# Fused attention and gated layers on one core: filler matmuls get steps and PSUM banks of their own

## Chip, cores, metric

One core of a Trainium2 chip. The metric is the device time of one execution in microseconds (us); three timed executions of the kernel before gave 471.35 us (median), 470.24 and 474.1 us.

## What is computed

The reference, cut to what matters (batch 8, 8 heads, 576 rows, head width 64, 32 packed rows, float32):

```python
def sm_attn(qq, kk, vv):
    s = scale * np.matmul(qq, kk.transpose(0, 1, 3, 2))
    s = s - np.max(s, axis=-1, keepdims=True)
    a = np.exp(s)
    a = a / (np.sum(a, axis=-1, keepdims=True) + 1e-09)
    return np.matmul(a, vv)
p_packed = sm_attn(p, k, v)
out = sm_attn(q, p_packed, p_packed)
...
x = np.ascontiguousarray(attn_out.transpose(0, 2, 1, 3)).reshape(B * S, H * D)
h = np.maximum(np.maximum(x @ w1, x @ w2), x @ w3)
return (h @ w_out).astype(np.float32)
```

## The kernel before

The work goes batch by batch (`b` 0 to 7). For a batch, `scores` multiplies the packed queries with the keys (line 255, `s<-kt`), `weigh` takes the maximum on VectorE (line 268) and the exponential on ScalarE (line 273), `turn` transposes the result on TensorE (lines 298 and 299, `tp`), `values` multiplies by the values (line 346), `packed` transposes the 32 packed rows (line 361), `queries` multiplies them with the queries (line 375, `s<-q`), `attend` does the second softmax, its scores being transposed out of PSUM by VectorE (line 398, `e<-s`). `project` multiplies the packed rows with the three first-layer weights of one block of 128 hidden columns (line 448, `pw`), split into a high part by ScalarE (line 459, `ph`) and a low part by VectorE (line 461, `pl`). `layer_in` applies that to the second softmax (line 484, `mi`: the bulk of the time), `maximum` combines the three sums, and `layer_out` does the output layer (line 553, `mo`).

`convert` unpacks the first-layer weights, which arrive as 64-bit words, in four steps: two on ScalarE (lines 190 and 195), one on VectorE (line 204), one on GpSimd (line 208).

The order of all work is written out by hand. Two strings are read word by word, START (batches 0 and 1 and the beginning of 2: the ramp) and LOOP (each further batch); nothing else orders the program. A word is one step of a stage. The first letter names the stage: `S` scores, `A` weigh and turn, `V` values, `K` packed, `Q` queries, `B` attend, `P` project, `N` layer_in, `E` maximum, `C` convert; digits are the batch and its part. Small letters issue loads on SyncE's queue (`k10` the keys of batch 1, first half; `w02` weights of block 0, part 2; `v`, `q` likewise). Each engine runs its own instructions in that order, so an instruction that waits holds up all behind it on its engine.

PSUM is given out from two pools: `ps_big` with two slots of two banks (scores, query scores, most projections) and `ps_moe` with four slots of one bank, tag `moe` (the layers' sums `mi` and `mo`, and, for batch 0, `tp`, `pa` and the first projection). A slot is given to a new tile when the last step that used the old tile stands earlier in the order; the first matmul of the new tile then waits for that step's instruction.

TensorE also does idle products, matmuls of the identity with itself that nobody reads. In the kernel before, a word `I10` only notes a number; the next stage that calls `rouse` issues that many products of 128 columns (at most four to a matmul) into the tile it is about to fill itself:

```python
if kind == "I":
    idle[0] = int(name[1:])
    continue
```

So the idle products wait for whatever that tile waits for, and stand between the wait and the stage's own matmuls. START has eight such words: I10 before `S0`, I10 and I1 before the two transposes of batch 0, I9 before `V00`, I2 before `Q0`, I5 before `S1` (the scores of batch 1), I3 before `S2`, I1 before `V101`.

Of the kernel before, what the change touches and what calls it, by code (L numbers as in the profile page):

```python
# [10 lines left out]
F32 = mybir.dt.float32  # L11
# [11 lines left out]
P = 128  # L23
# [22 lines left out]


START = """
k00 k01 I10 S0 A01 A01 I10 A01 A00 A00 v01 w00 C00 q010 v00 q000 A01 I1 A00 A00v C00 C00 I9 V00 Z00 q001 V00
V01 Z01 V01 K0 w01 K0v C01 I2 Q0 B010 B010 q011 Q0 C01 k11 k10 C01 B001 B001 B000 B011 B000 B011 w02 B000v  # L50
B011v C00 k21 B010 C01 B010 B010 B000 B000 B000v I5 S1 B011 k20 w12 C02 C02 I3 S2 B001 A10 B001 C02 C02 P00
B010v A11 A10 A11 B011 B010 B011 C12 B000 P00 B010g Z10 C12 B011 B010 w11 B010v B000g B000 v10 B001 A21 B001v
P00 P00 A11 Z11 B001 A20 B001g B011g B000v w10 v11 B000v A21 A10 B001 q10 C12 B001v A20 C10 N00 w21 B011 B010v
A10 A11 I1 V101 C10 B011 P00 N00 V101 C11 C11 B001v C11 C12 E000 q11 N00 C21 K1 C21 w20 N00 C10 K1v Q1 E000
E000 C20 C20 C21 w22 Z20 B011 N00 w30 B10 C22 C11 C10 P01 P01 N00 E001 w31 B11 B11 C21 C20 C20 C22 C22 C22 w50
C30 P01 w32 B10 C31 C30 P10 w41 X2 B10v N01 E010 C30 N01 C31 P02 P02 C31 w40 C32 N01 E001 E010 E001 C30 N01
N01 E011 C32 B11 C31 P02 C32 C32 E010 N02 v21 E011 N02 v20 N02 N02 w42 w52 B10 X2 H00 E020 E020 E020 B11 B11
B11v C40 C40 C40 C40 C41 C41 P03 N02 C41 P03 E021v P03 N01 N02 E021 w51 C42 C42 N03 N03 B10 X2 C41 B11 C52 B10
P10 w64 E011 C50 N03 C42 C42 E030v P10 H00 B10 Z21 N03 C52 P04 B11g P11 P04 E031 E021 E030 P04 N03 B10g w62
C52 N03 E030 N04 N04 E031 B11 C51 C51 B10 E040 E031 C52 E040 w65 H00 C50 B11 B11v P11 C51 N04 N04 B10 B10v N04  # L60
N04 E041 C64 C64 E041 E041 E040 C51 N10 C62 H02v E100 N10 N10 C50 C50 V201 q20 P11 P05 H03v w63 H02 C65 C65
C65 N11 E110 C64 C64 H03v C65 N11 N10 E100 V201 K2 E110 P05 C62 W2 N10 P05 E100 E101v C62 w60 H02v C63 N11
E110 H03v K2 q21 Q2 B21 N05 N05 C63 C63 B20 H01 E050 C63 N10 B20 B20 C60 P13 E050 W2 E101 C60 E101 P12 P13 W2
N05 H04v N05 P13 E050 C62 N11 E111 C60 N11 E111 B20 N11 W1v H03v P12 W1 P12 N13 E111 E051 N05 E051 H04 N05 N12
E051 C60 E130 N13 W1 N13 N12 W2 W2v P15 w61 C61 C61 C61 E120v E120 E130 P14 W1 W1v N13 C61 W0v W0v N12 E120
N12 W2 N13 H05g N12 W2 W2 P15 E130 H03 N12 E131 P15 B21 E121 E121 E131 P14 P14 N15 N15 N15 W0 N13 E150 E150
N14 N14 W2 N14 N14 N15 N15 E121 H03v H05 W2 W0 W0v E131 N14 W1 E150 E140 E140 E140 W0 W0 W0 H13 H04v H05 B20
E151v B20 O0 N14 E141v E141 E151 W1v N15 H01v E141 W0 k30 O0 F0 H10 O0 F0 O0 O0 O0 E151 H05v H10 W1 k31 P20
B20 H01 F0 H01v F0 W0v H10v P21 H05 B21v F0 H01 H05v P22 H01v F0 H12 H11 H14v O0 W1g H11v O0 H11v P21 B21 F0
O0 O0 H13 P20 P20 P20 H11v F0 H12 H12v B20 O0 F0 F0 F0 F0 H13 W1v P20 O0 B20 O0 O0 H14 F0 H14v F0 F0 B21 O1 F0  # L70
H15 H15v H15 O1 H11 B21 H13v F1 F1 H15v H15 H13v P22 O1 F1 H11v O1 H13v H15v O1 B20 F1 O1 O1 B20 O1 F1 B21
B21g P21 O1 O1 F1 F1 F1 F1 F1 F1 F1 P22 B21 O1 F1 O1 O1 F1 B21 B21 F1 O1 F1
"""


# [13 lines left out]
def fused_kernel(ctx: ExitStack, tc: tile.TileContext, kp, qt, va, vb, wi, wo, out):  # L89
# [19 lines left out]
    ps_moe = ctx.enter_context(tc.tile_pool(name="ps_moe", bufs=4, space=PSUM))  # L109
# [3 lines left out]
    ident = const.tile([P, P], F32, name="ident")  # L113
# [21 lines left out]
    def split_lo(lo, src, hi, default="g"):  # L135
        on(default).tensor_tensor(out=lo, in0=src, in1=hi.bitcast(F32), op=ALU.subtract)  # L136

    idle = [0]

    def rouse(ps):  # L140

        k = ps.shape[-1] // P
        for i in range(0, idle[0], k):
            n = min(idle[0] - i, k)
            nc.tensor.matmul(  # L145
                out=ps[:, 0:n * P], lhsT=ident, rhs=ident.unsqueeze(1).to_broadcast([P, n, P]),
                start=True, stop=True,
            )
        idle[0] = 0


    staged, loaded = {}, {}
    def load_w(j, c):
# [89 lines left out]
    s1, a1, z1, a1t, av, pp, s2, a2 = {}, {}, {}, {}, {}, {}, {}, {}  # L243

    def scores(b):

        kt = [loaded.pop(("k", b, g)) for g in range(G)]
        s1[b] = [ps_big.tile([P, 2, 512], F32, name=f"s1_{b}_{r}", tag="big") for r in range(R)]
        rouse(s1[b][0][:, 0])
        for hf in range(2):  # L250
            for n, (g, pr) in enumerate(QUADS):
                for r in range(R):
                    o = slice(64 * r, 64 * r + 64)
                    w = 2 * S + 64 * pr + 32 * r
                    nc.tensor.matmul(  # L255
                        out=s1[b][r][32 * n:32 * n + 32, hf, 0:HS],
                        lhsT=kt[g][o, w:w + NP],
                        rhs=kt[g][o, pr * S + hf * HS:pr * S + (hf + 1) * HS],
                        start=True, stop=True,
                    )  # L260
        yield 0
# [26 lines left out]
    def turn(b, r):  # L288
        if b == 0:
            tp = ps_moe.tile([P, 512], F32, name=f"tp{b}_{r}", tag="moe")  # L290
            pa = ps_moe.tile([P, 512], F32, name=f"pa{b}_{r}", tag="moe")
        else:
            x = ps_big.tile([P, 2, 512], F32, name=f"tp{b}_{r}", tag="big")
            tp, pa = x[:, 0], x[:, 1]
        a = a1[b, r][0]
        rouse(tp)
        for t in range(SF):
            nc.tensor.transpose(out=tp[:, t * P:(t + 1) * P], in_=a[:, t * P:(t + 1) * P], identity=ident)  # L298
        nc.tensor.transpose(out=pa[0:SR, 0:P], in_=a[:, SF * P:S], identity=ident)
        yield 2  # L300
        at = pool.tile([P, SF + 1, P], F32, name=f"a1t{b}_{r}", tag="b", bufs=NB)
        copy(at[:, 0:SF, :], tp.rearrange("p (t x) -> p t x", x=P))
        copy(at[0:SR, SF, :], pa[0:SR, 0:P])
        a1t[b, r] = at.rearrange("p t (i y) -> p t i y", y=NP)
        av[b, r] = pa
# [27 lines left out]
    def values(b, rs):  # L333

        at = {r: a1t.pop((b, r)) for r in rs}
        if (b, 0) not in av:
            x = ps_big.tile([P, 2, 512], F32, name=f"av{b}", tag="big")
            for r in range(R):
                av[b, r] = x[:, r]
        ps = {r: av[b, r][:, P:P + D] for r in rs}  # L340
        rouse(av[b, rs[0]][:, P:4 * P])
        for t, r in [(t, r) for ts in (range(SF), (SF,)) for r in rs for t in ts]:
            n = P if t < SF else SR
            for i, (g, pr) in enumerate(QUADS):
                h = 2 * pr + r
                nc.tensor.matmul(  # L346
                    out=ps[r][NP * i:NP * i + NP, :],
                    lhsT=at[r][0:n, t, i],
                    rhs=loaded["v", b, g][0:n, t, h * D:(h + 1) * D],
                    start=(t == 0), stop=(t == SF),  # L350
                )
        yield 1
        if b not in pp:
            pp[b] = pool.tile([P, R, D], F32, name=f"pp{b}", tag="pp", bufs=2)
        for r in rs:
            nc.vector.tensor_scalar(out=pp[b][:, r], in0=ps[r], scalar1=z1[b, r], scalar2=None, op0=ALU.mult)
# [8 lines left out]
    def queries(b):  # L365

        q = [loaded["q", b, g] for g in range(G)]
        s2[b] = []
        for hf in range(2):
            s2[b].append(ps_big.tile([P, R, 512], F32, name=f"s2_{b}_{hf}", tag="big"))  # L370
            rouse(s2[b][hf][:, 0])
            for n, (g, pr) in enumerate(QUADS):
                for r in range(R):
                    o = slice(64 * r, 64 * r + 64)
                    nc.tensor.matmul(  # L375
                        out=s2[b][hf][32 * n:32 * n + 32, r, 0:HS],
                        lhsT=pt_sb[b % 2][o, NP * n:NP * n + NP], rhs=q[g][o, pr, hf * HS:(hf + 1) * HS],
                        start=True, stop=True,
                    )
            if b == 0 or hf == 1:  # L380
                yield 0
# [51 lines left out]
    def project(b, j):  # L433
# [7 lines left out]
        else:  # L441
            x = ps_big.tile([P, R, 512], F32, name=f"pw{b}_{j}", tag="big")
            ps, src = [x[:, r] for r in range(R)], [x[:, :, 0:NW * P]]
        rouse(ps[0])
        for n in range(4):
            for r in range(R):
                o = slice(64 * r, 64 * r + 64)
# [20 lines left out]
    def layer_in(b, j):  # L468
# [3 lines left out]
        for hf in range(2):  # L472
            c = slice(hf * HS, (hf + 1) * HS)
            for i in range(NW):
                new = (range(NW) if i == 0 else ()) if first else (i,)
                for x in new:
                    sums[b, j, hf, x] = ps_moe.tile([P, 512], F32, name=f"mi{b}_{j}_{hf}_{x}", tag="moe")
                rouse(sums[b, j, hf, i])

                steps = [((2 * i + x) % 3, (2 * i + x) // 3) for x in range(2)] if first else [(i, 0), (i, 1)]  # L480
                for x, r in steps:
# [146 lines left out]
    def run(words, base):  # L628

        for word in words.split():  # L630
            name = word.rstrip("vga")
            chosen[0] = word[len(name):] or None
            kind, x = name[0], [int(i) for i in name[1:]]
            if kind == "I":
                idle[0] = int(name[1:])
                continue
            if kind not in "wCW":
                x[0] += base
# [58 lines left out]
```

## Time and profile before

| | us |
|---|---|
| median of 3 timed executions | 471.35 |
| lowest, highest of them | 470.24, 474.1 |
| the profiled execution, its own time | 474.43 |
| the span of the profiled execution | 472.7 |
| TensorE busy in that span | 457.1 |

The span runs from the first instruction to the last; 1.73 us of the profiled execution's time lie outside it. The profile says for each engine how long it was busy and what ended each of its idle times. The granted clock is TensorE's, as a share of 2.4 GHz: 1.00 is that level, 0.50 is 1.2 GHz.

### The profile page before, as it was taken

The numbers are of one execution on the slowest core, as the hardware profiler recorded it, in microseconds if no ns is written. First come the engines' busy times: TensorE is split into PE (matmuls) and PEld (weight loads), VectorE is DVE, ScalarE is ACT, GpSimd is POOL, SyncE is SP. The second block draws the span as 40 slices with busy tenths as digits, with TensorE's granted clock in tenths as the row PEclk, the third lists the DMA queues.
The fourth block names the chain that finished last, engine by engine and source line by source line (L and its number), as shares of the span: only waits on it lengthen the run. The fifth ranks groups of instructions, "written<-read, shape, count | busy, mean of one in ns | idle before, by whom it ended". The sixth has DMA issues, their size and how long they took to land.

```text
span 472.7 us, 11472 instructions
## 1 busy us (share of the span) xinstructions
PE 457.1 (97%) x4714; PEld 405.6 (86%) x4714; DVE 350.5 (74%) x763; ACT 171.8 (36%) x333; POOL 207.0 (44%) x180
## 2 busy tenths in 40 slices
PE   8769999999999999999999999999999999999996
PEld 4337887989899898989989898998989899898996
DVE  1677999999986678786777678786787767875652
ACT  3256876563441226122350224312260223402330
POOL 0335865766244046512564037521556036531642
PEclk9958999999999999999999999999999999999999
DMA  8995968003024730075102741057100910020002
GB/s 298 404 382 184 278 238 323 2 1 112 26 75 146 249 120 3 25 249 184 58 1 82 270 116 49 26 182 249 59 3 25 323 56 3 25 76 1 2 0 101
DMA packets 25540, 59.20 MB, mean 125 GB/s; under 512 B 2448, under 2 KB 15760, under 8 KB 25488
## 3 DMA queue, kind: packets, MB, share of 16 engines
q1 hardware_dynamic: 25488, 58.47, 36.3%
q8 instruction: 37, 0.61, 0.5%
q14 instruction: 15, 0.12, 0.1%
HBM read 45.48 MB, written 12.98 MB: 124 GB/s over the span
## 4 chain that ended last, share of the span: by engine, by line
PE 90%; DVE 4%; DMA 4%; ACT 1%; issue 1%; SPq 0%; DVEq 0%; ACTq 0%
PE mi L484 46%; PE mo L553 28%; PE pw L448 6%; PE s L255 2%; PE av L346 2%; PE s L375 2%; DMA wi<-in_wi 1%; DMA q<-in_qt 1%; DMA kt<-in_kp 1%; PE s L145 1%; DVE w_sb L204 1%; PE tp L145 1%; PE tp L298 1%; DVE e L398 1%; DVE xt L220 0%
## 5 line engine op out<-in xcount | busy, mean ns | idle before, releaser
L484 PE MATMUL mi<-a2h,ph 128*128 128x288 f32 x576 | 174.3, 303 | 0.7 <-ACT r L131 0.5
L484 PE MATMUL mi<-a2h,pl 128*128 128x288 f32 x576 | 170.3, 296 | 0.4 <-DVE pl L461 0.4
L484 PE MATMUL mi<-a2l,ph 128*128 128x288 f32 x576 | 170.2, 295 | 0.0
L484 PEld LDWEIGHTS mi<-a2h,ph 128*128 128x128 f32 x576 | 108.4, 188 | 16.1 <-issue 7.0
L484 PEld LDWEIGHTS mi<-a2h,pl 128*128 128x128 f32 x576 | 108.5, 188 | 0.6 <-DVE pl L461 0.6
L484 PEld LDWEIGHTS mi<-a2l,ph 128*128 128x128 f32 x576 | 108.4, 188 | 0.0
L498 DVE TENSOR_TENSOR r<-mi,r 128x288 f32<-128x288 f32 x192 | 83.3, 449 | 33.3 <-PE mi L484 31.2
L131 ACT COPY r<-mi 128x288 f32<-128x288 f32 x60 | 23.4, 400 | 123.3 <-PE mi L484 123.3
L461 DVE SCALAR_TENSOR_TENSOR pl<-pw,ph 128x768 fp32r<-128x768 f32 (+1 forms) x61 | 46.8, 775 | 3.9 <-ACT ph L459 3.0
L459 ACT ACTIVATE ph<-pw 128x768 fp32r<-128x768 f32 (+1 forms) x61 | 39.9, 675 | 21.8 <-PE pw L448 18.1
L553 PE MATMUL mo<-ych,xl 128*128 128x288 f32 x144 | 42.5, 295 | 0.0
L553 PE MATMUL mo<-ych,xh 128*128 128x288 f32 x144 | 42.4, 295 | 0.0
L553 PE MATMUL mo<-ycl,xh 128*128 128x288 f32 x144 | 42.4, 294 | 0.0
L136 POOL TENSOR_TENSOR yal<-r,yah 128x576 fp32r<-128x576 f32 x13 | 18.6, 1429 | 46.1 <-ACT yah L131 46.1
L448 PE MATMUL pw<-w_sb,pt 64*32 64x384 f32 x768 | 36.5, 495 | 1.0 <-POOL w_sb L208 1.0
L208 POOL TENSOR_TENSOR w_sb<-w_sb,wi 128x512 int32<-128x512 int32 x18 | 24.2, 1349 | 28.0 <-DVE z L284 11.7
L273 ACT ACTIVATE a<-s,nm 128x576 f32<-128x576 f32 x16 | 11.9, 743 | 67.3 <-DVE nm L269 67.1
L522 POOL TENSOR_TENSOR r<-r 128x288 f32<-128x288 f32 (+1 forms) x25 | 27.8, 1127 | 17.5 <-issue 9.0
L133 POOL CAST yah<-r 128x576 fp32r<-128x576 f32 x6 | 4.0, 663 | 57.0 <-DVE r L522 57.0
L553 PE MATMUL mo<-yah,xh 128*128 128x288 f32 x96 | 28.8, 300 | 0.0
L133 DVE COPY r<-mi 128x288 f32<-128x288 f32 x36 | 16.3, 455 | 16.2 <-PE mi L484 16.2
L553 PE MATMUL mo<-yal,xh 128*128 128x288 f32 x96 | 28.3, 295 | 0.0
(121 smaller groups left out, 883.6 us busy)
## 6 DMA issues: line engine op xcount, KB each, us to landing
kt<-in_kp SPq DMA_DIRECT2D x16, 640.0 KB, 4.7
wi<-in_wi SPq DMA_DIRECT2D x18, 512.0 KB, 7.0
v<-in_va SPq DMA_DIRECT2D x16, 512.0 KB, 5.9
q<-in_qt SPq DMA_DIRECT2D x14, 576.0 KB, 6.9
xk<-x SPq DMA_DIRECT2D x6, 576.0 KB, 4.9
wi<-in_wo SPq DMA_DIRECT2D x6, 512.0 KB, 5.7
out_t<-r SPq DMA_DIRECT2D x8, 288.0 KB, 2.2
out_t<-t SPq DMA_DIRECT2D x8, 288.0 KB, 2.3
```

Source lines behind the costliest of these rows:

```text
L131: e.copy(out=out, in_=src)
L133: e.tensor_copy(out=out, in_=src)
L136: on(default).tensor_tensor(out=lo, in0=src, in1=hi.bitcast(F32), op=ALU.subtract)
L208: nc.gpsimd.tensor_tensor(out=dst.bitcast(I32), in0=dst.bitcast(I32), in1=up, op=ALU.add)
L273: nc.scalar.activation(out=a.rearrange("p (a b) -> p a b", a=2), in_=s[:, :, 0:HS], func=AF.Exp, bias=nm, scale=SCALE, accum_out=z,)
L448: nc.tensor.matmul(out=ps[r][NP * n:NP * n + NP, 0:NW * P], lhsT=pt_sb[b % 2][o, NP * n:NP * n + NP], rhs=w_sb[o, j, n * NW * P:(n + 1) * ...
L459: nc.scalar.activation(out=hi[:, r], in_=x, func=AF.Copy, scale=2.0 ** -WS)
L461: nc.vector.scalar_tensor_tensor(out=lo[:, r], in0=x, scalar=2.0 ** -WS, in1=hi[:, r].bitcast(F32), op0=ALU.mult, op1=ALU.subtract,)
L484: nc.tensor.matmul(out=sums[b, j, hf, x][:, 0:HS], lhsT=w[:, r, x * P:(x + 1) * P], rhs=a[:, c], start=(r == 0 and n == 0), stop=(r == R - ...
L498: nc.vector.tensor_tensor(out=h, in0=sums[b, j, hf, i][:, 0:HS], in1=h, op=ALU.max)
L522: less = lambda out, x, y: on("g").tensor_tensor(out=out, in0=x, in1=y, op=ALU.subtract)
L553: nc.tensor.matmul(out=ps[:, 0:HS], lhsT=w[:, x, m * P:(m + 1) * P], rhs=h[:, z], start=(p == 0 and i == 0), stop=(p == NQ - 1 and i == 2),)
```

## The change

`rouse` and its calls go (lines 140 to 149 and the six stages that call it). A word `J<n>` takes their place and is a step of its own: it issues its products at once, each into a new tile of the pool `ps_moe`, 512 columns at most:

```diff
-    idle = [0]
-
-    def rouse(ps):
-        k = ps.shape[-1] // P
-        for i in range(0, idle[0], k):
-            n = min(idle[0] - i, k)
+    def doze(n):
+        for i in range(0, n, 4):
+            k = min(n - i, 4)
+            ps = ps_moe.tile([P, 512], F32, name=f"idle{len(dozes)}", tag="moe")
+            dozes.append(ps)
             nc.tensor.matmul(
-                out=ps[:, 0:n * P], lhsT=ident, rhs=ident.unsqueeze(1).to_broadcast([P, n, P]),
+                out=ps[:, 0:k * P], lhsT=ident, rhs=ident.unsqueeze(1).to_broadcast([P, k, P]),
                 start=True, stop=True,
             )
-        idle[0] = 0
+    dozes = []
...
-            if kind == "I":
-                idle[0] = int(name[1:])
+            if kind == "J":
+                doze(int(name[1:]))
                 continue
```

```diff
-k00 k01 I10 S0 A01 A01 I10 A01 A00 A00 v01 w00 C00 q010 v00 q000 A01 I1 A00 A00v C00 C00 I9 V00 Z00 q001 V00
+k00 k01 J10 S0 A01 A01 J7 A01 A00 A00 v01 w00 C00 q010 v00 q000 A01 A00 A00v C00 C00 J1 V00 Z00 q001 V00 V01 Z01
```

START now has J10 before `S0`, J7 before the first transpose of batch 0, J1 before `V00`, before `K0`, before `Q0` and between the two halves of `Q0`, J11 before `S1`, J12 before `S2`, J8 and J1 before the two transposes of batch 1, J1 before `Q1`, J2 before the projection `P01`, J6 before `N01` (the second layer block of batch 0). Together 62 products of 128 columns where 41 stood. All other words keep their order, on every engine and on the load queue, and LOOP is unchanged.

TensorE's rows before the values of batch 0 (`pa<-v`), with the semaphores that they wait for, before and after:

```order
L299 MATMUL pa_0_147<-ident,a_0_0_127 64x128
L145 MATMUL pa_0_147<-ident 128x384 [waits DVE_49]
L145 MATMUL pa_0_147<-ident 128x384 x2
L346 MATMUL pa_0_147<-v_138,a1t_0_154 32x64 [waits DMAHW6_49]
L346 MATMUL pa_0_147<-v_138,a1t_0_154 32x64
```

```order
L296 MATMUL pa_0_151<-ident,a_0_0_131 64x128 [waits PE_49]
L144 MATMUL idle_162<-ident 128x128 [waits Activation_49]
L342 MATMUL pa_0_151<-v_142,a1t_0_157 32x64 [waits DMAHW6_49,DVE_49]
L342 MATMUL pa_0_151<-v_142,a1t_0_157 32x64
L342 MATMUL pa_0_151<-v_134,a1t_0_157 32x64 [waits DMAHW2_49]
```

Three matmuls, 1152 columns, went; one of 128 columns stands there, and the wait for VectorE's copy (`DVE_49`) moved from the first idle product to the first product of the values.

TensorE's rows from the second half of the query scores of batch 0 (`s<-q`) to the scores of batch 1 (`s<-kt`), before and after:

```order
L375 MATMUL s_0_1_232<-q_136,pt_75 32x288 [waits DMAHW3_49]
L375 MATMUL s_0_1_232<-q_136,pt_75 32x288 x3
L145 MATMUL s_1_0_273<-ident 128x512 [waits DVE_49,PE_49]
L145 MATMUL s_1_0_273<-ident 128x128
L255 MATMUL s_1_0_273<-kt_244 32x288 [waits DMAHW5_49]
L255 MATMUL s_1_1_274<-kt_244 32x288 [waits DVE_49,PE_49]
```

```order
L370 MATMUL s_0_1_239<-q_140,pt_75 32x288 [waits DMAHW3_49]
L370 MATMUL s_0_1_239<-q_140,pt_75 32x288 x3
L144 MATMUL idle_280<-ident 128x512 [waits PE_49]
L144 MATMUL idle_282<-ident 128x512 [waits PE_49]
L144 MATMUL idle_284<-ident 128x384
L253 MATMUL s_1_0_286<-kt_251 32x288 [waits DMAHW5_49,DVE_49,PE_49]
L253 MATMUL s_1_1_287<-kt_251 32x288 [waits DVE_49,PE_49]
```

The idle products (640 columns, now 1408) no longer stand behind the wait for VectorE (its transposes out of the slot that the scores take); they wait only for earlier idle products of TensorE itself, and the scores carry the wait.

TensorE's rows from the projection of batch 1 (`pw_0_616`, then `pw_0_641`) to the block `N01` (`mi_1_0_0`), before and after:

```order
L448 MATMUL pw_0_616<-w_sb,pt_76 32x384 [waits DVE_49,PE_49]
L448 MATMUL pw_0_616<-w_sb,pt_76 32x384 x7
L484 MATMUL mi_1_0_0_633<-a2h_0_400,ph_1_583 128x288 [waits Activation_49]
L484 MATMUL mi_1_0_0_633<-a2h_0_400,pl_1_584 128x288 [waits DVE_49]
L484 MATMUL mi_1_0_0_633<-a2l_0_407,ph_1_583 128x288
```

```order
L442 MATMUL pw_0_641<-w_sb,pt_76 32x384 [waits DVE_49,PE_49]
L442 MATMUL pw_0_641<-w_sb,pt_76 32x384 x7
L144 MATMUL idle_658<-ident 128x512 [waits PE_49]
L144 MATMUL idle_660<-ident 128x256 [waits Activation_49]
L477 MATMUL mi_1_0_0_662<-a2h_0_420,ph_1_608 128x288 [waits PE_49]
L477 MATMUL mi_1_0_0_662<-a2h_0_420,pl_1_609 128x288 [waits DVE_49]
```

Two idle products, 768 columns, stand where none stood; the second waits for the ScalarE copy that frees its bank, for which the block's second sum waited before.

## Rows read from the trace of the kernel before

**Rows 1.** The page: span, TensorE's busy time, its granted clock in 40 slices.
```profile
span 472.7 us, 11472 instructions
...
PE 457.1 (97%) x4714; PEld 405.6 (86%) x4714; DVE 350.5 (74%) x763; ACT 171.8 (36%) x333; POOL 207.0 (44%) x180
...
PEclk9958999999999999999999999999999999999999
```

**Rows 2.** Windows: length, busy us by engine (instructions), granted clock, DMA share, GB/s.
```profile
18.40:22.10 3.70, 1.36 (x14) 0.78 (x20) 3.63 (x11) 0.46 (x2) 2.65 (x3) 1.00 1.03 413
22.10:39.20 17.10, 12.85 (x164) 7.67 (x163) 12.43 (x37) 11.52 (x27) 6.09 (x7) 0.50 0.97 362
...
48.00:60.00 12.00, 12.00 (x113) 10.20 (x105) 11.56 (x28) 9.84 (x18) 9.54 (x9) 1.00 0.92 289
...
100.00:200.00 100.00, 99.78 (x957) 93.19 (x957) 81.44 (x164) 35.29 (x68) 45.43 (x40) 1.00 0.27 89
```

**Rows 3.** Timeline of TensorE in the ramp: start, us, what [idle before <-releaser].
```profile
12.14 2.20 PE L145 MATMUL pa<-ident 128*128 128x384 f32 x6 [0.86 <-DVE a1t L133]
14.27 1.73 PE L346 MATMUL pa<-v,a1t 128*32 128x64 f32 x80
...
17.21 1.21 PE L375 MATMUL s<-q,pt 64*32 64x288 f32 x32
20.75 1.32 PE L145 MATMUL s<-ident 128*128 128x512 f32 x4 [2.34 <-DVE e L398]
22.00 2.10 PE L255 MATMUL s<-kt 64*32 64x288 f32 x32
26.07 1.65 PE L145 MATMUL s<-ident 128*128 128x384 f32 x2 [1.97 <-ACT a L273]
27.64 2.17 PE L255 MATMUL s<-kt 64*32 64x288 f32 x32
29.57 1.53 PE L448 MATMUL pw<-w_sb,pt 64*32 64x384 f32 x16
33.38 1.11 PE L298 MATMUL tp<-ident,a 128*128 128x128 f32 x4 [2.28 <-ACT a L273]
...
37.57 2.22 PE L346 MATMUL tp<-v,a1t 128*32 128x64 f32 x80
...
42.41 1.20 PE L375 MATMUL s<-q,pt 64*32 64x288 f32 x32
...
45.58 0.88 PE L448 MATMUL pw<-w_sb,pt 64*32 64x384 f32 x16 [0.97 <-POOL w_sb L208]
...
47.39 0.88 PE L448 MATMUL pw<-w_sb,pt 64*32 64x384 f32 x16
48.20 0.40 PE L484 MATMUL mi<-a2h,ph 128*128 128x288 f32 x1
```

**Rows 4.** Timeline of SyncE, ScalarE and VectorE in the ramp, same columns.
```profile
9.81 1.13 SPq L161 DMA_DIRECT2D kt<-in_kp  x2
...
12.22 0.33 SPq L155 DMA_DIRECT2D wi<-in_wi  x1
...
22.80 0.66 ACT L190 ACTIVATE wi<-wi 128x512 f32<-128x512 f32 x1
...
25.18 0.74 ACT L273 ACTIVATE a<-s,nm 128x576 f32<-128x576 f32 x1 [0.83 <-DVE nm L269]
...
26.46 0.74 ACT L273 ACTIVATE a<-s,nm 128x576 f32<-128x576 f32 x1 [0.45 <-DVE nm L269]
...
33.47 0.74 ACT L273 ACTIVATE a<-s,nm 128x576 f32<-128x576 f32 x1
...
41.93 0.94 DVE L498 TENSOR_TENSOR r<-mi,r 128x288 f32<-128x288 f32 x2
```

**Rows 5.** DMA issues of 10.2 to 11.5 us, then 12 to 16: KB, us to landing.
```profile
kt<-in_kp SPq DMA_DIRECT2D x1, 640.0 KB, 9.7
...
wi<-in_wi SPq DMA_DIRECT2D x1, 512.0 KB, 9.3
```

More of the change, by code (lines that the diff above doesn't have):

```diff
@@ L48 @@
 START = """
-k00 k01 I10 S0 A01 A01 I10 A01 A00 A00 v01 w00 C00 q010 v00 q000 A01 I1 A00 A00v C00 C00 I9 V00 Z00 q001 V00
[L50 to L72, printed above, removed]
+k00 k01 J10 S0 A01 A01 J7 A01 A00 A00 v01 w00 C00 q010 v00 q000 A01 A00 A00v C00 C00 J1 V00 Z00 q001 V00 V01 Z01
@@ new lines @@
+V01 J1 K0 w01 K0v C01 J1 Q0 B010 B010 q011 J1 Q0 C01 k11 k10 C01 B001 B001 B000 B011 B000 B011 w02 B000v B011v
+C00 k21 B010 C01 B010 B010 B000 B000 B000v J11 S1 B011 k20 w12 C02 C02 J12 S2 B001 A10 B001 C02 C02 P00 B010v
+A11 A10 A11 B011 B010 B011 C12 B000 P00 B010g Z10 C12 B011 B010 w11 B010v B000g B000 v10 B001 A21 B001v P00 P00
+J8 A11 Z11 B001 A20 B001g B011g B000v w10 v11 B000v A21 J1 A10 B001 q10 C12 B001v A20 C10 N00 w21 B011 B010v A10
+A11 V101 C10 B011 P00 N00 V101 C11 C11 B001v C11 C12 E000 q11 N00 C21 K1 C21 w20 N00 C10 K1v J1 Q1 E000 E000 C20
@@ new lines @@
+C20 C21 w22 Z20 B011 N00 w30 B10 C22 C11 C10 J2 P01 P01 N00 E001 w31 B11 B11 C21 C20 C20 C22 C22 C22 w50 C30 P01
+w32 B10 C31 C30 P10 w41 X2 B10v J6 N01 E010 C30 N01 C31 P02 P02 C31 w40 C32 N01 E001 E010 E001 C30 N01 N01 E011
+C32 B11 C31 P02 C32 C32 E010 N02 v21 E011 N02 v20 N02 N02 w42 w52 B10 X2 H00 E020 E020 E020 B11 B11 B11v C40 C40
+C40 C40 C41 C41 P03 N02 C41 P03 E021v P03 N01 N02 E021 w51 C42 C42 N03 N03 B10 X2 C41 B11 C52 B10 P10 w64 E011
+C50 N03 C42 C42 E030v P10 H00 B10 Z21 N03 C52 P04 B11g P11 P04 E031 E021 E030 P04 N03 B10g w62 C52 N03 E030 N04
@@ new lines @@
+N04 E031 B11 C51 C51 B10 E040 E031 C52 E040 w65 H00 C50 B11 B11v P11 C51 N04 N04 B10 B10v N04 N04 E041 C64 C64
+E041 E041 E040 C51 N10 C62 H02v E100 N10 N10 C50 C50 V201 q20 P11 P05 H03v w63 H02 C65 C65 C65 N11 E110 C64 C64
+H03v C65 N11 N10 E100 V201 K2 E110 P05 C62 W2 N10 P05 E100 E101v C62 w60 H02v C63 N11 E110 H03v K2 q21 Q2 B21
+N05 N05 C63 C63 B20 H01 E050 C63 N10 B20 B20 C60 P13 E050 W2 E101 C60 E101 P12 P13 W2 N05 H04v N05 P13 E050 C62
+N11 E111 C60 N11 E111 B20 N11 W1v H03v P12 W1 P12 N13 E111 E051 N05 E051 H04 N05 N12 E051 C60 E130 N13 W1 N13
@@ new lines @@
+N12 W2 W2v P15 w61 C61 C61 C61 E120v E120 E130 P14 W1 W1v N13 C61 W0v W0v N12 E120 N12 W2 N13 H05g N12 W2 W2 P15
+E130 H03 N12 E131 P15 B21 E121 E121 E131 P14 P14 N15 N15 N15 W0 N13 E150 E150 N14 N14 W2 N14 N14 N15 N15 E121
+H03v H05 W2 W0 W0v E131 N14 W1 E150 E140 E140 E140 W0 W0 W0 H13 H04v H05 B20 E151v B20 O0 N14 E141v E141 E151
+W1v N15 H01v E141 W0 k30 O0 F0 H10 O0 F0 O0 O0 O0 E151 H05v H10 W1 k31 P20 B20 H01 F0 H01v F0 W0v H10v P21 H05
+B21v F0 H01 H05v P22 H01v F0 H12 H11 H14v O0 W1g H11v O0 H11v P21 B21 F0 O0 O0 H13 P20 P20 P20 H11v F0 H12 H12v
@@ L73 @@
+B20 O0 F0 F0 F0 F0 H13 W1v P20 O0 B20 O0 O0 H14 F0 H14v F0 F0 B21 O1 F0 H15 H15v H15 O1 H11 B21 H13v F1 F1 H15v
+H15 H13v P22 O1 F1 H11v O1 H13v H15v O1 B20 F1 O1 O1 B20 O1 F1 B21 B21g P21 O1 O1 F1 F1 F1 F1 F1 F1 F1 P22 B21
+O1 F1 O1 O1 F1 B21 B21 F1 O1 F1
 """
@@ L248, in scores @@
         s1[b] = [ps_big.tile([P, 2, 512], F32, name=f"s1_{b}_{r}", tag="big") for r in range(R)]
-        rouse(s1[b][0][:, 0])
         for hf in range(2):
@@ L295, in turn @@
         a = a1[b, r][0]
-        rouse(tp)
         for t in range(SF):
@@ L340, in values @@
         ps = {r: av[b, r][:, P:P + D] for r in rs}
-        rouse(av[b, rs[0]][:, P:4 * P])
         for t, r in [(t, r) for ts in (range(SF), (SF,)) for r in rs for t in ts]:
@@ L370, in queries @@
             s2[b].append(ps_big.tile([P, R, 512], F32, name=f"s2_{b}_{hf}", tag="big"))
-            rouse(s2[b][hf][:, 0])
             for n, (g, pr) in enumerate(QUADS):
@@ L443, in project @@
             ps, src = [x[:, r] for r in range(R)], [x[:, :, 0:NW * P]]
-        rouse(ps[0])
         for n in range(4):
@@ L477, in layer_in @@
                     sums[b, j, hf, x] = ps_moe.tile([P, 512], F32, name=f"mi{b}_{j}_{hf}_{x}", tag="moe")
-                rouse(sums[b, j, hf, i])
                 steps = [((2 * i + x) % 3, (2 * i + x) // 3) for x in range(2)] if first else [(i, 0), (i, 1)]
```

## The prediction

> **What bounds the kernel now.** I read the page first. TensorE is busy for 457.1 of 472.7 us, and its granted clock is full in all slices but two near the start [rows 1]. The windows say where the missing time lies. From 48 to 60 us TensorE is busy for all of the 12.00 us, and from 100 to 200 us for 99.78 of 100 [rows 2]: there it is the bound, and what TensorE reaches earlier at 48 us should end earlier at the end. What can be won lies in the ramp. From 22.10 to 39.20 us the clock was 0.50, that is 1.2 GHz, for 17.10 us; in the 3.70 us before it fell, TensorE was busy for 1.36 us [rows 2]. The timeline of TensorE shows that stretch: it waited 2.34 us for VectorE's transposes, then did 1.32 us of idle products, and only then the scores of batch 1, `S1` [rows 3]. So the idle products did not fill the wait, they followed it. In the half-clock stretch DMA is busy 0.97 of the time and VectorE for 12.43 of 17.10 us [rows 2]; neither gets faster with TensorE's clock.
>
> **The change, part by part.** All times here are of the profiled execution, 474.43 us, of which 472.7 are the span.
>
> Price of a product: three idle matmuls of 384 columns took 2.20 us at full clock [rows 3], 1.9 ns a column. So J11 costs 2.7 us, J12 2.9, J8 1.95, J6 1.46, J2 0.5, J1 0.24; at half clock twice that.
>
> 1. I9 before `V00` (2.20 us) becomes J1. The values and all up to the query scores `Q0` (17.21 us) can come about 2 us earlier. The wait of J1 for ScalarE's copy is not new in effect: the values wait for a copy of the same steps.
> 2. `S1` began at 22.00 us [rows 3]. With 2 us gained and I5 out of the path it would begin near 18.8, but its keys are the second of two loads issued from 9.81 us, at about 10.6 [rows 4], and took 9.7 us to land [rows 5]: 20.3. The load queue is in the same order and DMA moves 413 GB/s at share 1.03 [rows 2], so I leave that landing where it is. J11 runs from about 16.3 to 19.0, inside the wait. `S1` begins at 20.3.
> 3. At full clock `S1` takes 1.2 us, as the query scores of the same shape do, instead of 2.10 [rows 3]. It ends at 21.5 instead of 24.1: 2.6 us earlier.
> 4. `S2` waits for ScalarE's two exponentials of `S1`, the last ending at 27.20 [rows 4]. Before them ScalarE has the conversion of weights that are issued at 12.22 and land 9.3 us later, at 21.5 [rows 4, 5]; it began at 22.80, so only 1.3 us can be gained by it. From there to 27.20 are 4.40 us, with 0.83 and 0.45 us of waiting for VectorE [rows 4]. If both waits go, the exponentials end at 24.6, if both stay at 25.9; I take 25.1, since VectorE is busy 3.63 of 3.70 us just before [rows 2]. `S2` begins at 25.1 instead of 27.64, 2.5 us earlier; J12 ends before, at 24.4.
> 5. `S2` takes 1.2 instead of 2.17 us, the projection behind it 0.88 instead of 1.53 [rows 3]: 1.6 more, 4.1 us in all at 27.0.
> 6. From the projection's end (31.1) to the end of batch 1's values (39.8) are 8.7 us. TensorE at full clock saves half of the transposes (twice four, 1.11 us each four) and 0.5 of 2.22 on the values, which took 1.73 at full clock [rows 3]: 1.6 us; the sums between them save a little more, at most 0.4 by the same halving. The exponentials (the last starts at 33.47 [rows 4]) and VectorE stand between and stay as long; I take 1.5. J8 fits in the wait of 2.28 us [rows 3]. Sum: 5.6 us earlier at the end of the values. Bounds: 4.1 and 6.1.
> 7. J1 before `Q1` waits for VectorE's first maximum. That pair started at 41.93 and took 0.94 us for two, so the first was over at 42.40, and `Q1` began at 42.41 [rows 3, 4]: nothing. Behind it on TensorE stand all later products, so a late maximum would delay them one for one, by up to 0.5 us. J2 before `P01` lies in the wait of 0.97 us [rows 3]: nothing.
> 8. J6 before `N01` has no cover in this trace. The projection in front of it started at 47.39 and took 0.88, `N01` began at 48.20 [rows 3]: no gap. If ScalarE and VectorE, which make `N01`'s operands, come out as far ahead as TensorE, J6 costs its 1.46 us; if they are late, down to nothing. I take 1.3.
>
> Sum: 5.6 - 1.3 = 4.3 us, 470.1 instead of 474.43 us for an execution like the profiled one. Behind 48 us nothing changes in kind, and I carry the 4.3 us through.
>
> **From the profiled execution to the median.** The three timed executions spread over 3.9 us, about as much as the half-clock stretch costs, and the profiled one is slower than the slowest. Either profiling costs 3.1 us always (then 467.0), or the median execution has lost less to the clock (then the gain there is small, and 470.1 stands). No row decides; I take the middle, 468.6 us.
>
> The Trainium skill (TensorE: Matmul & The Clock Gate, Part 1) says that the clock's monitor runs free of the program, so that one kernel gets its clock at different points from run to run. By that rule the spread is the clock's, and the result would be 470.1. The one trace of before cannot show it; the spread of the three times agrees with it.
>
> **Rivals.**
>
> *Little is left to win (470.8, no change).* Either most executions lose less to the clock than the profiled one, or DMA holds the ramp: steps 2 and 4 both stop at a landing, and the same can happen to later loads. Then the gain is what the moved fillers give without a clock difference, at most the 1.32 us in front of `S1` and part of the 1.65 in front of `S2` [rows 3], say 1.9, less J6: 0.6 us from the median. For it: DMA share 0.97 in the half-clock stretch. Against it: TensorE's work there is longer by the clock alone, and 17.10 us at half clock is the largest single thing in the ramp.
>
> *The clock falls earlier (slower, 474.4).* The 1152 columns before `V00` kept TensorE busy; now, from the end of J7 near 9.1 us to J11 near 16.3, there are only transposes, small products and J1s with waits between. If the clock drops there, the large fillers run at half clock on the path: J11 5.2 us instead of 2.7, so it ends at 21.7; `S1` takes 2.10, to 23.8; J12 5.0 (some of it back at full clock), to 28.8, past the point where the exponentials release `S2`; `S2` and the projection 3.7, to 32.5; J8 up to 3.9. The transposes that began at 33.38 would come 2 to 3 us later, and J6 adds 1.3; less what an earlier return of the clock gives back, 3 us: 471.35 + 3.0. It decides if the clock is at half when J11 starts. For it: the clock fell once where TensorE was busy 1.36 of 3.70 us. Against it: in before it held through waits of 0.86 us and 0.97 us [rows 3], and most of the new waits are no longer than that.
>
> *The banks bind (471.4).* Idle products take slots of the sums' pool, so a step could wait for a slot that a filler holds, and the change would fill the gaps and lose as much. Against it: nobody reads the fillers, so their slots are free at once; only two of them wait for VectorE's maxima and one late one for ScalarE's copy, each priced above.
>
> **How the numbers follow.** Forecast 0.50 (465.5 to 471), little left 0.27, clock falls earlier 0.13, banks 0.10. About 1% is what a measurement of this kernel can tell from no change, so faster by over 1% means under 466.6: that takes the whole 3.1 us of profiling cost and a J6 that hides; I give it 0.23, nearly all out of the forecast's half. Slower by over 1% (476.1) needs the clock lost and not regained before J6: 0.05. The range is from 465.0 (467.0 with J6 hidden and 0.7 more from step 6) to 473.0, which leaves out the worse half of the third case.
>
> **What would show it.** Right: granted clock 1.00 from 18 to 45 us; `S1` at 20.3 with DMA as its releaser, 1.2 us long; `S2` near 25; `P01` near 40; two idle matmuls of together 1.5 us with no wait before `N01`. Wrong: half clock anywhere between 10 and 40 us, J12 still running when the exponentials of `S1` are over, or gaps of TensorE between 48 and 60 us that before did not have, which would mean that loads or VectorE could not follow.

## The result: 4.0 us less, within one per cent

| | us |
|---|---|
| before, median of 6 executions | 472.05 (470.24 to 474.1) |
| changed, median of 6 | 468.01 (467.84 to 468.29) |
| ratio, 95% interval | 0.9915 (0.9891 to 0.994) |
| changed, profiled execution; its span | 468.03; 466.2 |

The forecast was 468.6, the range 465.0 to 473.0. The gain is under 1%; to a time within 1% of before the prediction gave 0.72. The changed kernel repeats to 0.45 us where before spread over 3.9.

The page of the changed kernel, the lines of [rows 1]:

```profile
span 466.2 us, 11503 instructions
...
PE 457.3 (98%) x4728; PEld 405.3 (87%) x4728; DVE 349.8 (75%) x763; ACT 172.6 (37%) x333; POOL 207.1 (44%) x180
...
PEclk9999999999999999999999999999999999999999
```

TensorE is busy as long as before, with 21 products more of filler; the clock's two lower digits near the start are gone. The windows of [rows 2], in the changed kernel:

```profile
18.40:22.10 3.70, 2.84 (x37) 1.33 (x36) 3.22 (x10) 1.38 (x3) 1.30 (x2) 1.00 1.03 415
22.10:39.20 17.10, 16.09 (x217) 10.20 (x215) 16.00 (x47) 13.47 (x31) 9.75 (x10) 1.00 1.02 385
48.00:60.00 12.00, 12.00 (x121) 10.08 (x120) 10.38 (x28) 10.70 (x19) 8.94 (x8) 1.00 0.78 277
```

Where TensorE was busy for 1.36 us before the clock fell it is now busy for 2.84, and the clock stays at 1.00 through the 17.10 us that had run at 0.50. VectorE, busy 12.43 us of that stretch before, is now busy 16.00: the same work comes earlier. The timeline of TensorE, the lines that answer to [rows 3]:

```profile
11.65 0.49 PE L144 MATMUL idle<-ident 128*128 128x128 f32 x2 [0.27 <-ACT a1t L131]
12.24 1.73 PE L342 MATMUL pa<-v,a1t 128*32 128x64 f32 x80
...
16.24 0.72 PE L370 MATMUL s<-q,pt 64*32 64x288 f32 x16
16.88 2.63 PE L144 MATMUL idle<-ident 128*128 128x512 f32 x6
20.37 1.32 PE L253 MATMUL s<-kt 64*32 64x288 f32 x32 [0.86 <-DMA kt<-in_kp]
21.63 2.84 PE L144 MATMUL idle<-ident 128*128 128x512 f32 x6
24.81 1.35 PE L253 MATMUL s<-kt 64*32 64x288 f32 x32 [0.35 <-DMA kt<-in_kp]
25.78 1.03 PE L442 MATMUL pw<-w_sb,pt 64*32 64x384 f32 x16
26.74 1.98 PE L144 MATMUL idle<-ident 128*128 128x512 f32 x4
29.09 0.66 PE L295 MATMUL tp<-ident,a 128*128 128x128 f32 x4 [0.36 <-ACT a L271]
...
31.94 1.66 PE L342 MATMUL tp<-v,a1t 128*32 128x64 f32 x80
...
39.56 0.88 PE L442 MATMUL pw<-w_sb,pt 64*32 64x384 f32 x16 [0.29 <-POOL w_sb L207]
...
41.37 0.88 PE L442 MATMUL pw<-w_sb,pt 64*32 64x384 f32 x16
42.17 1.56 PE L144 MATMUL idle<-ident 128*128 128x512 f32 x4
43.38 0.48 PE L477 MATMUL mi<-a2h,ph 128*128 128x288 f32 x1
...
78.77 1.52 PE L442 MATMUL pw<-w_sb,pt 64*32 64x384 f32 x32
```

J11 (16.88), J12 (21.63) and J8 (26.74) end before what they precede is released, so the waits at their ends are short, 0.86, 0.35 and 0.36 us, where TensorE had waited 2.34, 1.97 and 2.28 [rows 3]. The lead over before is 3.8 us at the first projection (25.78 against 29.57), 6.0 at `P01` (39.56 against 45.58) and 4.8 at `N01` behind J6 (43.38 against 48.20).

Against this profile of before it does not stay at 4.8. Two later waits of that execution were for a late operand; its timeline:

```profile
60.63 0.40 PE L484 MATMUL mi<-a2h,pl 128*128 128x288 f32 x1 [0.39 <-DVE pl L461]
...
81.52 1.17 PE L375 MATMUL s<-q,pt 64*32 64x288 f32 x24 [0.20 <-DMA q<-in_qt]
...
85.20 1.52 PE L448 MATMUL pw<-w_sb,pt 64*32 64x384 f32 x32
```

In the changed kernel neither wait exists between 43 and 100 us; the only entry of its waits there is 0.2 us for VectorE's maximum. The second line's 0.20 understates its wait: the weight load ahead of it waited 0.7 us for the same load of queries (issued at 75.87, landed 5.6 us later; in the changed kernel issued at 70.30 and landed in 4.6). Projections behind these two places lead by 5.55 (58.37 against 63.92) and 6.43 us (78.77 against 85.20), and the end by 6.5 (466.2 against 472.7). Whether the change removed these two waits, or whether they belong to this one execution of before, the second profile of before tells (first experiment below).

### The profile page after: what moved, and what is told of

Its sections match the earlier page's. It is cut to its first block, busy times and chain, and to the rows that moved or that the text cites. A ratio compares the mean times of both kernels' runs of the same rounds, so it can differ in the third digit from the quotient of the medians.

```text
span 466.2 us, 11503 instructions
## 1 busy us (share of the span) xinstructions
PE 457.3 (98%) x4728; PEld 405.3 (87%) x4728; DVE 349.8 (75%) x763; ACT 172.6 (37%) x333; POOL 207.1 (44%) x180
## 4 chain that ended last, share of the span: by engine, by line
PE 92%; DVE 4%; DMA 2%; ACT 0%; issue 0%; POOL 0%; POOLq 0%; ACTq 0%
PE mi L477 49%; PE mo L546 29%; PE pw L442 7%; DMA kt<-in_kp 2%; PE s L253 2%; PE av L342 2%; PE s L370 1%; PE idle L144 1%; DVE mx L266 1%; DVE xt L219 0%; DVE w_sb L203 0%; DVE r L491 0%; ACT a L271 0%; PE tp L342 0%; DVE xl L136 0%
## 5 line engine op out<-in xcount | busy, mean ns | idle before, releaser
L546 PE MATMUL mo<-ybh,xl 128*128 128x288 f32 x96 | 28.3, 295 | 0.0
```

The lines of the kernel that those rows point to most:

```text
L546: nc.tensor.matmul(out=ps[:, 0:HS], lhsT=w[:, x, m * P:(m + 1) * P], rhs=h[:, z], start=(p == 0 and i == 0), stop=(p == NQ - 1 and i == 2),)
```

## Experiments

All times are medians; the executions of before that ran beside them are given where they are compared.

**The kernel before, profiled again.** No edit.

> The kernel before, unchanged, profiled a second time. Theory A (the executions of before differ in how long TensorE runs at half clock in the ramp, since the clock's monitor runs free of the program): the half-clock stretch starts, ends or is absent at another place than 22.16 to 39.22 us, and the span differs from 472.7 by 1 to 3 us with the difference made before 48 us. Theory B (profiling or something else makes the spread): the same stretch to within 0.5 us, whatever the time.

Measured: 470.65 us, span 468.8, 3.9 under the first profile. Windows and TensorE's timeline of this execution:

```profile
21.00:25.90 4.90, 2.88 (x38) 1.17 (x36) 4.80 (x16) 3.40 (x8) 1.91 (x3) 1.00 1.02 410
25.90:29.40 3.50, 3.50 (x49) 1.36 (x48) 2.69 (x10) 1.17 (x4) 1.37 (x3) 0.51 1.05 370
29.40:32.80 3.40, 1.06 (x13) 0.50 (x5) 2.72 (x11) 2.86 (x7) 1.40 (x2) 1.00 1.02 359
32.80:36.20 3.40, 3.24 (x18) 2.98 (x22) 3.21 (x7) 2.55 (x9) 1.30 (x1) 0.50 1.02 411
```

```profile
20.71 1.32 PE L145 MATMUL s<-ident 128*128 128x512 f32 x4 [2.34 <-DVE e L398]
21.96 1.20 PE L255 MATMUL s<-kt 64*32 64x288 f32 x32
25.18 0.93 PE L145 MATMUL s<-ident 128*128 128x384 f32 x2 [2.02 <-ACT a L273]
26.04 2.59 PE L255 MATMUL s<-kt 64*32 64x288 f32 x32
27.96 1.73 PE L448 MATMUL pw<-w_sb,pt 64*32 64x384 f32 x16
...
45.97 0.40 PE L484 MATMUL mi<-a2h,ph 128*128 128x288 f32 x1
...
81.38 1.52 PE L448 MATMUL pw<-w_sb,pt 64*32 64x384 f32 x32
```

The same program up to 22 us (`S1` at 21.96 against 22.00), but here `S1` runs at full clock, and half clock is granted in two pieces, 25.9 to 29.4 and 32.8 to 36.2, instead of one of 17.10 us. That much of theory A holds: the half clock moves from execution to execution. Its second half does not: 1 to 3 us were expected, all of it before 48 us, and of the measured 3.9 only 2.2 lie before `N01` (45.97 against 48.20). The other 1.7 lie between 48 and 86 us: neither the wait for `pl` nor the one for the load of queries stands in this execution. So these two waits came with the first execution and are no fixed part of the kernel before. Against this second profile the lead of the changed kernel is 2.6 us at `N01` (43.38 against 45.97), 2.6 behind the queries (78.77 against 81.38) and 2.6 at the end (466.2 against 468.8): it is carried through unchanged.

The 23 executions of before in this comparison, grouped by the mean granted clock of each:

```
clock   executions   us (mean)
0.982   2            473.75
0.989   4            472.88
0.993   7            471.04
0.996   4            469.31
```

(6 with clocks between these are left out.) Not one execution of before had more than 0.996. The time goes with the clock, 4.4 us from the lowest group to the highest; whether late operands, as in the first profile, come with a low clock or by chance is open. The first profile (474.43, clock 0.982) was slower than all 23.

**Without J6.**

```diff
-w32 B10 C31 C30 P10 w41 X2 B10v J6 N01 E010 C30
+w32 B10 C31 C30 P10 w41 X2 B10v N01 E010 C30
```

> The changed kernel without the six products before N01. Theory A (they lie on TensorE's path, 1.33 us, and all behind is bound by TensorE): 1.0 to 1.3 us faster than the changed kernel, 466.7 to 467.0. Theory B (what is gained there is lost in the next waits for operands or loads): the time of the changed kernel, 468.0, with new idle time of TensorE between 44 and 80 us.

Measured: 466.97 us (466.57 to 467.56), clock 0.999 or more in all six; ratio to before 0.9911 (0.9876 to 0.9946). Repeated beside the changed kernel on one chip, both unchanged:

> The changed kernel, unchanged, timed beside the one without J6 on one chip. Theory A (the clock is held whatever the phase of its monitor): all executions within 1 us of each other, near 468.0, granted clock 0.998 or more in each, while those of before spread over 4 us. Theory B (it was luck in the first six): some executions at 0.996 or less and 469 or more.

> The changed kernel without J6, on the same chip. Theory A (J6 is on the path and holds nothing): 0.8 to 1.3 us under the changed kernel, clock as high. Theory B (J6 costs nothing in the median): within 0.4 us.

Measured: 468.33 (468.05 to 469.13) with J6, 467.01 (466.7 to 467.16) without, clock 0.998 or more in all twelve; before 471.82 there, its clock 0.982 to 0.996. J6 costs 1.3 us, its own length on the path (the block behind J6 began at 43.38, 1.2 us after J6 at 42.17), and protects nothing. Without it the kernel beats both: 0.9895 of before (0.9875 to 0.9916). Theory A in all three, with one small miss: the six executions with J6 spread over 1.08 us where at most 1 was expected. The one at 469.13 had a clock of 1.0, so not all of the remaining spread is the clock.

**Old counts, new place.** The changed kernel's steps and banks with the words of before:

```diff
-C01 J1 Q0 ... J11 S1 ... J12 S2 ... J8 A11 ... J6 N01
+C01 J2 Q0 ... J5 S1 ... J3 S2 ... A11 ... N01
```

> The changed kernel's way of issuing (own steps, own banks) with the old words' counts and places: 41 products instead of 62, J9 before V00, J5 before S1, J3 before S2, none before the transposes of batch 1 and none before N01. Theory A (out of the waits is one half of the gain, the longer fillers are what holds the clock): the clock falls near 22 us as before, S1 starts at 20.3 but the projection and transposes run at half clock: 469.5 to 471.5. Theory B (only the place matters): the clock holds and without J6 the time is 466.5 to 467.5.

Measured: 470.15 us (469.06 to 470.89, 12 executions), ratio 0.9976 (0.9956 to 0.9997). Windows:

```profile
20.00:25.30 5.30, 2.89 (x36) 1.13 (x36) 5.17 (x18) 3.54 (x8) 2.24 (x3) 1.00 1.02 411
25.30:28.80 3.50, 3.12 (x46) 1.09 (x46) 2.68 (x8) 1.12 (x4) 1.30 (x2) 0.51 1.04 364
28.80:32.10 3.30, 0.96 (x12) 0.50 (x5) 2.58 (x10) 2.85 (x7) 1.40 (x2) 1.00 1.02 354
32.10:35.60 3.50, 3.33 (x24) 3.08 (x27) 3.22 (x7) 2.65 (x9) 1.30 (x1) 0.51 1.02 411
```

and the scores of batch 1 in the same execution:

```profile
20.13 1.41 PE L253 MATMUL s<-kt 64*32 64x288 f32 x32 [1.22 <-DMA kt<-in_kp]
```

The clock falls, at 25.3 here and not at 22, and in all 12 executions the mean clock is 0.996 or less. At a clock of 0.993 this kernel's mean is 470.29 (8 executions) against 471.04 for before, at 0.996 469.24 against 469.31: the place alone is worth under 1 us. `S1` starts at 20.13, no later than in the changed kernel.

**New counts, old place.** The kernel before with the new words, issued by `rouse` into the stage's tile (the one before `K0` is lost, since that stage does not call `rouse`):

```diff
-I5 S1 ... I3 S2 ... A11 ... N01
+I11 S1 ... I12 S2 ... I8 A11 ... I6 N01
```

> The old way of issuing (into the stage's own tile, behind its wait) with the new words and counts, one product lost before K0. Theory A (the place beside the waits matters): the clock holds, but J11, J12 and J8 follow their waits, 2.6, 2.8 and 2.0 us on the path, less what later waits take up: 472 to 476. Theory B (only the clock matters): full clock from 7 us on and 467 to 469.

Measured: 473.91 us (472.4 to 476.55, 12 executions), ratio 1.0052 (1.0026 to 1.0078): slower. The window of the first filler, and TensorE:

```profile
18.80:22.00 3.20, 3.19 (x4) 1.49 (x5) 2.58 (x8) 1.49 (x4) 0.99 (x2) 0.50 1.03 415
23.00:60.00 37.00, 31.71 (x389) 21.85 (x389) 30.17 (x79) 24.53 (x50) 19.79 (x18) 1.00 0.85 299
```

```profile
18.81 4.20 PE L145 MATMUL s<-ident 128*128 128x512 f32 x6 [1.76 <-DVE e L398]
22.94 1.20 PE L255 MATMUL s<-kt 64*32 64x288 f32 x32
26.15 2.84 PE L145 MATMUL s<-ident 128*128 128x512 f32 x6 [2.01 <-ACT a L273]
28.93 1.20 PE L255 MATMUL s<-kt 64*32 64x288 f32 x32
29.92 0.85 PE L448 MATMUL pw<-w_sb,pt 64*32 64x384 f32 x16
33.05 1.98 PE L145 MATMUL tp<-ident 128*128 128x512 f32 x4 [2.28 <-ACT a L273]
```

The three waits are back, and the fillers follow them: 4.20 us (most of it at half clock), 2.84 and 1.98. From 23 us on the clock is full, `S2` and the projection take 1.20 and 0.85, and still the kernel is slower than before. Theory A has the time right, but not its "the clock holds": the mean clock was 1.00 in only three of the twelve executions and 0.992 to 0.996 in the others. In those three it took 472.7. Theory B, that the clock alone matters, is out.

**One long filler less.** Each of J11, J12, J8 taken out of the kernel without J6:

```diff
-... J11 S1 ... J12 S2 ... J8 A11 ... J6 N01
+one of J11, J12, J8 left out, and J6
```

> The changed kernel without J6 and without J11, so that TensorE is idle from the query scores of batch 0 (16.7 us) to the scores of batch 1 (20.1). Theory A (each long filler holds the clock by itself): the clock falls between 18 and 23 us in most executions, S1, the projection or J12 run at half clock: 468 to 471, and the executions differ by 1 us or more. Theory B (one filler of two is enough): 466.6 to 467.4, full clock throughout.

> The changed kernel without J6 and without J12, so that TensorE waits some 3.2 us between the scores of batch 1 and of batch 2. Theory A: the clock falls between 23 and 27 us in most executions; S2, the projection and the transposes at half clock cost 1 to 3 us: 468 to 470. Theory B (J11 is enough): 466.6 to 467.4.

> The changed kernel without J6 and without J8, so that TensorE waits 2.3 us before the transposes of batch 1. Theory A: in some executions the clock falls near 28 to 31 us, transposes and values then lose up to 1.6 us: median 467 to 468.5 with a spread over 1 us. Theory B (the wait is too short to matter, what was done around it holds the clock): 466.6 to 467.4.

Measured: 468.49 (467.8 to 469.56) without J11, 468.39 (466.87 to 469.22) without J12, 467.57 (466.71 to 468.12) without J8, against 466.97 with all three. The windows at and behind the gap that each leaves, in this order:

```profile
16.00:20.40 4.40, 1.34 (x31) 0.48 (x18) 3.95 (x11) 1.33 (x3) 2.65 (x3) 1.00 1.02 408
20.40:23.90 3.50, 3.45 (x34) 1.86 (x35) 2.33 (x8) 2.41 (x6) 0.00 (x0) 0.51 1.02 413
```

```profile
25.70:29.20 3.50, 3.50 (x33) 1.21 (x18) 3.02 (x12) 2.32 (x5) 0.17 (x2) 0.51 1.06 364
29.20:40.00 10.80, 10.54 (x162) 8.01 (x160) 10.15 (x25) 8.85 (x19) 7.44 (x7) 1.00 0.99 372
```

```profile
29.10:32.50 3.40, 3.17 (x15) 3.09 (x16) 3.33 (x9) 2.01 (x6) 2.25 (x3) 0.50 1.03 360
32.50:40.00 7.50, 7.50 (x146) 6.08 (x145) 6.21 (x15) 6.60 (x14) 4.60 (x5) 1.00 0.95 365
```

Each time the clock falls within 1.0 us of the gap's end (without J12, `S2` still begins at full clock), and a stage behind it runs at half clock: `S1`, then `S2`'s projection, then the transposes. In each of the three profiles it stayed there for one such stretch. In 19 of these 20 executions the mean clock was 0.992 to 0.996, once 0.999; so each of the three is needed to hold the clock. In time the fillers are worth 1.5, 1.4 and 0.6 us, but these three kernels ran on another chip than the 466.97, beside executions of before of 472.64 and not 471.53. On their own chip only `lean` below had all three long fillers, at 467.42: leaving out J11 or J12 costs 1.1 or 1.0 us against that, and J8's 0.15 us is inside the spread.

**The small fillers out as well** (`lean`). J2 and the J1s before `K0`, at `Q0` (two), between the two transposes of batch 1 and before `Q1`, besides J6. The expectation names the J1 between the transposes as kept; the edit took it out too. Part of the edit:

```diff
-V01 Z01 V01 J1 K0 w01 K0v C01 J1 Q0 B010 B010 q011 J1 Q0 C01
+V01 Z01 V01 K0 w01 K0v C01 Q0 B010 B010 q011 Q0 C01
```

> The changed kernel with J10, J7, J1 before the values, J11, J12, J8 and J1 between the transposes alone: without J6, J2 and the J1s before K0, in and before Q0 and before Q1. Theory A (small fillers lie in waits or before work that waits for a landing anyway, and the large ones hold the clock): 466.4 to 467.1, the same as without J6 alone. Theory B (the small fillers bridge the stretch from 9 to 16 us and keep the clock up there): the clock falls near 12 to 19 us in some executions, 467.5 to 470.

Measured: 467.42 us (466.77 to 468.46), clock 0.998 or more in all six. The clock does not need them. But the times lie no lower, 0.4 us above the kernel without J6 in the median (timed on another chip) and above the 466.4 to 467.1 expected, inside that kernel's range in part, so nothing is won either. The first two lines show why the ramp wins nothing: the projection `P01` waits for its weights from GpSimd and starts at 39.61 us, first here, then in the repeated run without J6. The third, from the waits of 43 to 100 us, shows where the profiled execution (468.46) loses:

```profile
39.61 0.88 PE L442 MATMUL pw<-w_sb,pt 64*32 64x384 f32 x16 [1.15 <-POOL w_sb L207]
39.61 0.88 PE L442 MATMUL pw<-w_sb,pt 64*32 64x384 f32 x16 [0.26 <-POOL w_sb L207]
PE s L370 <- DMA q<-in_qt: 0.7, 1, 0.7
```

The load of queries that the first profile of before waited for at 81 us is late here too, at 75.5. From the start of these query scores to the projection behind them this execution took 5.06 us. The same stretch took 4.57 and 3.71 us in the two profiles of before, and 3.70 and 4.20 in the two of the changed kernel: the load is early or late from execution to execution of one program. Whether taking the small fillers out makes it late more often is open, since the other five executions were not profiled.

## Why the prediction was right, step by step

*Half clock as the largest thing in the ramp.* Shown by the two mixed kernels. At the old counts the place gains 1.4 us in the median (471.53 to 470.15), under 1 at equal clock; at the old place the new counts lose 2.4 us (473.91); both together gain 3.5 to 4.0, and 4.6 to 4.8 without J6. From the old counts in the new place to the kernel without J6, on one chip, it is 3.2 us (470.15 to 466.97). `S1` began no earlier for it (20.13 and 20.14), so it is won behind `S1`, where the clock differs. The fillers must be long enough to hold the clock, and they may only be that long where they stand in a wait. The place in the order and the own bank were always changed together; which of the two a kernel needs was not tested.

*Step 2, 4 and 5, the places where the ramp stops.* `S1` began at 20.37 with DMA as its releaser (20.3 was said). The exponentials: ScalarE's timeline of the changed kernel, the lines that answer to [rows 4]:

```profile
21.53 0.67 ACT L189 ACTIVATE wi<-wi 128x512 f32<-128x512 f32 x1 [0.67 <-DMA wi<-in_wi]
...
24.09 0.74 ACT L271 ACTIVATE a<-s,nm 128x576 f32<-128x576 f32 x1 [0.27 <-DVE nm L267]
```

ScalarE waits for the weights to 21.53 (21.5 was said), and the second exponential ends at 24.83 (25.1). `S2` began at 24.81, the projection ended at 26.8 (27.0). One thing I had wrong there: the trace names the keys' load, not the exponentials, as what `S2` waited for last (0.35 us); both came within 0.1 us of each other.

*Step 6.* The values of batch 1 ended at 33.6, 6.2 us earlier; I took 5.6 with 6.1 as the upper bound. From the first transpose on it took TensorE 4.51 us instead of 6.41, 1.9 less where I took 1.5 of at most 2.0: ScalarE and VectorE held up less than I let them.

*Step 7.* J1 before `Q1` and J2 cost nothing in the end, but not for the reason given. `Q1` does come later by its J1: 36.72 in the repeated run without J6, 36.27 in `lean`, in both behind products that end together. `P01` takes up this 0.45 us, since it waits for its weights to 39.61 in both; so "would delay them one for one" was wrong. No wait of a step names a bank of a filler.

*Step 8.* J6: 1.3 said, 1.2 in the trace, 1.3 in the direct comparison.

*"Behind 48 us nothing changes in kind, and I carry the 4.3 us through".* At `N01` the lead over the first profile was 4.8 us, 0.5 more than the 4.3 of the sum; all of it had come by the end of step 6. Behind it the lead over that profile grew by 1.6 us, through the two late operands. But the second profile of before has neither wait, and against it the lead is 2.6 us at `N01` and at the end. So the step holds for the change; what it missed is that the first profile carried 1.6 us of loss of its own behind 48 us. [rows 2] has no row between 60 and 100 us, where I would have seen it. Profile against profile the change is worth 6.4 us (474.43 to 468.03) or 2.6 (470.65 to 468.03), in the medians 3.5 to 4.0.

*"No row decides; I take the middle": luck.* Profiling does not cost 3.1 us: the second profile of before (470.65) lies under the median beside it, the changed kernel's on its median (468.03 and 468.01). The other branch was nearer, but the first profile was slow for two reasons, 2.2 us of clock in the ramp and 1.7 us behind it, each measured against the second. By that branch my sum would have given 470.1, 2.1 us too slow: 0.5 are missing in the ramp, 1.6 behind it. Taking off half of the 3.1 us happened to make up 1.5 of them. The mechanism in the ramp was right in its main steps; that 468.6 came so close to 468.01 is luck. The rule of the Trainium skill (TensorE: Matmul & The Clock Gate, Part 1), that the clock's monitor runs free of the program, agrees with the second profile of before: half clock at other places of the same program, at 25.9 and not at 22.16.

*The rivals.* "Little is left to win" was right in one condition: 21 of the 23 executions of before lost less clock than the profiled one (0.982). But all of them lost some, 0.996 at best, and the gain was 3.5 to 4.0 us and not 0.6. Loads do end the waits before `S1` and `S2`, by only 0.86 and 0.35 us. "The clock falls earlier" fails: in the changed kernel all twelve executions had 0.998 or more, and without the small fillers too the stretch from 9 to 16 us kept its clock. (In that rival J11 at half clock is 5.4 us by my own price, which gives its 21.7, and not 5.2.) "The banks bind" found no wait of a step for a filler.

## What to carry to other kernels

A filler matmul belongs in the wait, in a buffer of its own and ahead of the instruction that waits; the same filler behind the wait is added to the path, here enough to turn a gain of 4 us into a loss of 2.4. Length it to the wait, and leave out one without a wait: J6 cost its whole length on the path. Before pricing a change in a ramp, profile the kernel before twice and compare the granted clock of several executions: one profile may be the worst of them, and a wait that only one of two profiles shows is not the change's to win.

## What the runs showed of the hardware that was not expected

The same program loses its clock at different points: 17.10 us in one piece in one execution, 3.5 and 3.4 us with full clock between in another; means from 0.982 to 0.996 go with 473.75 to 469.31 us. With a wait of TensorE of 2.26 us before the transposes (J8 out) the profile shows half clock behind it, and four of five executions lost clock (0.996); the same wait with 1.98 us of fillers in it left the clock at 0.998 or more in all. No such wait decides alone: in the second profile of before, `S1` ran at full clock behind a wait of 2.34 us.
